# Windowed attention feeding a dense layer: attention in groups of 128 queries with four-tile scores, instead of tiles of 64

## The chip, the cores and the metric

The kernel runs on one core of one Trainium2 chip. The metric is the device time of one execution in microseconds. Before the change three runs gave 781.32, 781.82 and 783.75 us, with a median of 781.82.

The core has a matrix engine (TensorE, PE; its weight loads are counted apart as PEld), a vector engine (VectorE, DVE), an activation engine (ScalarE, ACT), GpSimd (POOL) and SyncE (SP), which here issues all DMAs of data.

## The reference

There are 4 batches, 8 heads, 768 tokens and a head size of 64. Each query sees the keys less than 16 tokens away, and one summary per block of 32 tokens: the maximum of the keys and the mean of the values. The attention's result, 3072 x 512, goes through a gated layer of width 1536:

```
k_sum = k.reshape(B, H, 24, 32, D).max(axis=3)
v_sum = v.reshape(B, H, 24, 32, D).mean(axis=3)
scores_l = where(abs(i - j) < 16, scale * q @ k.T, -1e9)
scores_s = scale * q @ k_sum.T + log(32)
a = softmax(concat(scores_l, scores_s))
x = (a @ concat(v, v_sum)).transpose(0, 2, 1, 3).reshape(3072, 512)
out = ((x @ w_a) * (x @ w_b)) @ w_out
```

q, k and v are fp32. The weights come as 64-bit floats and are converted on the chip.

## The kernel before, in words

**The dense layer.** The 3072 tokens are 12 units u of 256 rows, three to a batch. The hidden width is 12 blocks f of 128. A pair (u, f) is an item; there are 144. `hidden` multiplies the unit's x by a block of w_a and of w_b (`up`, 12 matmuls of 128x256 each, L487; three products per 128 rows, since x and the weights are split into a high and a low part). ACT copies the first product to SBUF (L521), DVE multiplies the second into it (L522, the tensor g), ACT rounds g to its high part gh (L525), POOL makes the low part gl (L526). `down` then adds g @ w_out to the unit's two PSUM banks po with 6 matmuls of 128x512 (L504). It runs one item late: the program issues the up matmuls of item i, then the down matmuls of item i - 1. The PSUM tile h of an item has two buffers, so the up matmuls of an item wait for the g of two items before.

**Order of the items.** Units 0 and 1 are interleaved (five items of unit 0, then one of unit 1 and one of unit 0 in turn), because each item there also needs its weights converted: 36 conversions of 128x512 (L168 to L192) on ACT, DVE and POOL, each using two tiles of the pool `stage`, 7 buffers, and the PSUM tile psc. Units 2 to 11 follow one after the other.

**Attention.** `attention(u)` is a generator; the main loop takes its steps between the matmuls of the items of unit u - 1, spread evenly by `a_steps` (14 steps, or 20 for the first unit of a batch). All of unit 0's attention stands at the start. On every engine a scheduler then sets the final order.

A unit's 256 queries are 4 tiles of 64 (QT). Of a tile:
- `prep_q` turns q so that the head dimension lies on partitions and writes it to a block-diagonal tile qbd (two heads of 64 rows, zeros elsewhere); by DVE block transposes from a load in 32x32 blocks (L369), or, for units 0 to 2 (u < FILL), by TensorE and ACT copies (L367).
- `scores` multiplies it with 120 keys, 96 of the window and 24 summaries that lie between the window's two halves in the key tile kT: 4 matmuls of 128x120 on the full array (L385). DVE scales and masks (L391) and takes the maximum (L397), ACT does 4 exps (L399), DVE the reciprocal of the sums (L403, L404), POOL the division (L409).
- `transp` turns the weights of attention with 16 DVE transposes of 32x128 (L426), or for u < FILL on TensorE (L419), and the value sums are loaded into the value tile vw by a DMA.
- `av` multiplies with vw: 8 matmuls of 120x64, each in one half of the array's columns (L434). ACT and DVE write the high and low part of x (L439, L440).

`load_v` loads the window's values with two DMAs into vw (L375), which has two buffers. `prep_k` runs at the start of a batch: it loads keys in 32x32 blocks (L295), transposes them into kT (L327), takes block maxima (L328) and has POOL write the summaries between the windows (L332). `sum_v` (L229 to L237) makes the value means. All DMAs of the blocks of k and q wait for the last weight conversion.

Of the kernel before, what the change touches and what calls it, by code (L numbers as in the profile page):

```python
# [21 lines left out]
def attention_moe(  # L22
# [21 lines left out]
    KEYS = NS + WIN  # L44
    CH = 256
    NR = S // CH
    G = CH // QT
# [3 lines left out]
    stage = ctx.enter_context(tc.tile_pool(name="stage", bufs=7))  # L51
# [16 lines left out]
    PAIR = 2 * QT + NS  # L68

    def window(t):  # L70

        if t == 0:
            return 0, QT
        if t == S // QT - 1:
            return S - WIN, WIN - QT
        return QT * t - 16, 16 if t % 2 else WIN - 16

    def column(token):
        return PAIR * (token // (2 * QT)) + (QT + NS) * (token // QT % 2) + token % QT

    kinds = {0: 0, S // QT - 1: 3}
    mask = const.tile([P, 4, KEYS], F32, name="mask")
    nc.gpsimd.memset(mask, 0.0)
    for i, t in enumerate((0, 1, 2, S // QT - 1)):
        start, na = window(t)
        off = QT * t - start
        for h in range(2):
            hs = slice(h * QT, (h + 1) * QT)  # L90
            for c0, n, key in ((0, na, 0), (na + NS, WIN - na, na)):
                sl = mask[hs, i, c0 : c0 + n]

                for sign, base in ((1, 15 - off + key), (-1, 15 + off - key)):
                    nc.gpsimd.affine_select(
                        out=sl,
                        in_=sl,
                        compare_op=ALU.is_ge,
                        fill=NEG,
                        base=base,  # L100
                        pattern=[[sign, n]],
                        channel_multiplier=-sign,
                    )
        nc.gpsimd.memset(mask[:, i, na : na + NS], LOG32)


    qbds = []
    for i in range(2):
        t = const.tile([P, NP, P], F32, name=f"qbd{i}")
        nc.vector.memset(t, 0.0)  # L110
        qbds.append(t)
# [5 lines left out]

    sbufs = []
    for i in range(2):
        t = const.tile([P, NP, P], F32, name=f"s{i}")  # L120
        nc.gpsimd.memset(t[:, :, KEYS:], 0.0)
        sbufs.append(t)

# [72 lines left out]
    kTs, vsums = {}, {}  # L196
# [57 lines left out]
    def load_first():  # L254
# [14 lines left out]
        first["v"].append(att.tile([P, S], F32, tag="kin", name="v_in2", bufs=1)[:, :512])  # L269
        first["v"].append(stage.tile([P, 512], F32, tag="t2k", name="v_in3"))  # L270
        first["v"] += [att.tile([P, 512], F32, tag="pt", name=f"v_in{4 + i}") for i in range(2)]
# [14 lines left out]
    def blocks(dst, x, b, c, row):  # L286

        for h in range(2):
            for e in range(D // 32):
                src = x[b, 2 * c + h, row:, e * 32 :]
                r0 = 32 * (2 * h + e)
                load = nc.sync.dma_start(  # L295
                    out=dst[r0 : r0 + 32].rearrange("p (n d) -> p n d", d=32),
                    in_=bass.AP(
                        tensor=src.tensor,
                        offset=src.offset,
                        ap=[[D, 32], [32 * D, dst.shape[1] // 32], [1, 32]],  # L300
                    ),
                )
                tc.add_manual_dep(load.ins, converted[-1].ins.name, after, reason="pace")

    def prep_k(b, early):
        kT = att.tile([P, NP, S // P, PAIR], F32, tag="kT", name=f"kT{b}", bufs=1)
        ks = att.tile([P, NP, NS], F32, tag="ksum", name=f"ks{b}", bufs=1)
        n = P // BLK
        if early:
            for i in range(S // P):  # L310
                tr = turned(first["k"][i], f"k{i}", 0)
                nc.scalar.copy(out=kT[:, :, i, :QT], in_=tr[:, :, :QT])
                nc.scalar.copy(out=kT[:, :, i, QT + NS :], in_=tr[:, :, QT:])
# [6 lines left out]
        for c in range(NP):  # L320
            if not early:
                xin = att.tile([P, S], F32, tag="kin", name=f"kin{b}_{c}", bufs=1)
                blocks(xin, k, b, c, 0)
                xin = xin.rearrange("p (i e x) -> p e i x", e=2, x=QT)
                kv = ks[:, c, :].rearrange("p (i e n) -> p e i n", e=2, n=QT // BLK)
                for e, half in enumerate((kT[:, c, :, :QT], kT[:, c, :, QT + NS :])):
                    nc.vector.transpose(out=half, in_=xin[:, e])  # L327
                    nc.vector.tensor_reduce(  # L328
                        out=kv[:, e], in_=half.rearrange("p i (n x) -> p i n x", x=BLK),
                        axis=AX.X, op=ALU.max,  # L330
                    )
            nc.gpsimd.tensor_copy(  # L332
                out=kT[:, c, :, QT : QT + NS],
# [4 lines left out]
        kTs[b] = kT.rearrange("p c n x -> p c (n x)")  # L338
# [17 lines left out]
    def prep_q(u, i, qin):  # L356
        if u < FILL:
            x = turned(qin[:, i, :], f"q{u}_{i}", u)
        else:
            x = qin[:, :, i * P : i * P + P]  # L360
        for j in range(2):
            for h in range(2):
                hs = slice(h * D, (h + 1) * D)
                dst = qbds[j][hs, :, h * QT : (h + 1) * QT]
                src = x[hs, :, j * QT : (j + 1) * QT]
                if u < FILL:
# [46 lines left out]
    def transp(b, t, u):  # L413
# [10 lines left out]
        for qs in blk:  # L424
            for ks in blk:
                nc.vector.transpose(out=ptv[ks, :, qs], in_=s[qs, :, ks])  # L426
# [187 lines left out]
```

## Time and profile before

| what | value |
|---|---|
| median of three runs | 781.82 us (781.32 to 783.75) |
| the profiled execution | 783.04 us, span 781.2 us |
| mean granted TensorE clock | 0.984 |
| PE busy | 726.3 us, 93% of the span |
| DVE busy | 505.7 us, 65% |
| ACT busy | 278.1 us, 36% |
| POOL busy | 250.6 us, 32% |
| first item's matmuls start | 48.7 us |
| first items of units 2, 3 and 11 | 189.8, 256.7 and 728.2 us |

The starts of units are those of the first w_a or w_b run of their item 0 in the trace. The time of an execution is 1.8 us longer than its span. Busy PE time contains some overlap and some modelled ends, so times of matmuls are better read from the start of one run to the start of the next in the timeline. A group of instructions is printed as line, engine, operation, output<-inputs, sizes and count, then its total busy time and the mean ns of one, then the idle time just before and what ended it. A wait is printed as engine and tile, what it waited for, and total us, times, longest.

### The profile page before, as it was taken

The numbers are of one execution on the slowest core, as the hardware profiler recorded it, in microseconds if no ns is written. First come the engines' busy times: TensorE is split into PE (matmuls) and PEld (weight loads), VectorE is DVE, ScalarE is ACT, GpSimd is POOL, SyncE is SP. The second block draws the span as 40 slices with busy tenths as digits, with TensorE's granted clock in tenths as the row PEclk, the third lists the DMA queues.
The fourth block names the chain that finished last, engine by engine and source line by source line (L and its number), as shares of the span: only waits on it lengthen the run. The fifth ranks groups of instructions, "written<-read, shape, count | busy, mean of one in ns | idle before, by whom it ended". The sixth has DMA issues, their size and how long they took to land.

```text
span 781.2 us, 14975 instructions
## 1 busy us (share of the span) xinstructions
PE 726.3 (93%) x5580; PEld 655.4 (84%) x5580; DVE 505.7 (65%) x1262; ACT 278.1 (36%) x898; POOL 250.6 (32%) x328
## 2 busy tenths in 40 slices
PE   6668998999789999999999999999989999999997
PEld 4367888888678989988888989988988989989996
DVE  4779999834884664767867665667876656556100
ACT  4758965423222322322222422322223332322212
POOL 5567789921222212212222221222122221121111
PEclk9869999999999999999999999999999999999999
DMA  9965645246411211204521111114421111100000
GB/s 217 219 191 164 172 136 176 85 86 137 91 30 31 55 21 39 50 18 86 138 36 39 50 31 27 49 32 75 126 37 27 55 35 29 43 13 14 28 1 28
DMA packets 157129, 56.97 MB, mean 73 GB/s; under 512 B 136704, under 2 KB 148992, under 8 KB 157056
## 3 DMA queue, kind: packets, MB, share of 16 engines
q1 hardware_dynamic: 157056, 56.01, 29.8%
q8 instruction: 44, 0.72, 0.4%
q14 instruction: 29, 0.24, 0.1%
HBM read 47.19 MB, written 6.29 MB: 68 GB/s over the span
## 4 chain that ended last, share of the span: by engine, by line
PE 40%; DVE 33%; ACT 7%; POOL 5%; SPq 5%; DMA 4%; issue 4%; ACTq 0%; DVEq 0%; POOLq 0%
PE h L487 23%; DVE ptsb L426 15%; PE po L504 13%; ACT s L399 5%; POOL s L409 3%; DVE vp L230 3%; SPq L295 2%; DVE s L391 2%; DVE nml L397 2%; PE av L434 2%; DVE qbd L369 2%; PE s L385 2%; DMA kin<-in_k_dram 2%; DVE g L522 2%; DVE kT L327 1%
## 5 line engine op out<-in xcount | busy, mean ns | idle before, releaser
L487 PE MATMUL h<-x,w_a 128*128 128x256 f32 x1728 | 247.3, 284 | 15.4 <-DVE g L522 14.4
L487 PEld LDWEIGHTS h<-x,w_a 128*128 128x128 f32 x1728 | 231.3, 190 | 33.6 <-DVE g L522 17.9
L487 PE MATMUL h<-x,w_b 128*128 128x256 f32 x1728 | 225.4, 278 | 0.0
L487 PEld LDWEIGHTS h<-x,w_b 128*128 128x128 f32 x1728 | 211.7, 189 | 1.8 <-POOL w_b L192 0.2
L526 POOL TENSOR_TENSOR gl<-g,gh 128x256 fp32r<-128x256 f32 x144 | 106.0, 738 | 324.1 <-ACT gh L525 316.4
L426 DVE STREAM_TRANSPOSE ptsb<-s 32x128 f32<-32x128 f32 x576 | 174.3, 303 | 32.2 <-POOL s L409 23.3
L504 PE MATMUL po<-w_o,gh 128*128 128x512 f32 x576 | 171.6, 404 | 6.2 <-ACT gh L525 5.6
L522 DVE TENSOR_TENSOR g<-h,g 128x256 f32<-128x256 f32 x144 | 59.8, 419 | 116.1 <-ACT g L521 114.6
L525 ACT CAST gh<-g 128x256 fp32r<-128x256 f32 x144 | 58.2, 407 | 182.5 <-DVE g L522 182.4
L504 PEld LDWEIGHTS po<-w_o,gh 128*128 128x128 f32 x576 | 97.7, 188 | 24.5 <-ACT gh L525 10.3
L521 ACT COPY g<-h 128x256 f32<-128x256 f32 x144 | 52.4, 369 | 171.0 <-PE h L487 169.2
L399 ACT ACTIVATE s<-s,nml 128x120 f32<-128x120 f32 x192 | 73.5, 384 | 91.5 <-DVE nml L397 91.4
L504 PE MATMUL po<-w_o,gl 128*128 128x512 f32 x288 | 100.1, 398 | 0.7 <-POOL gl L526 0.2
L409 POOL TENSOR_TENSOR s<-s,nml 128x480 f32<-128x480 f32 x40 | 39.5, 988 | 106.6 <-DVE nml L404 67.8
L385 PE MATMUL s<-kT,qbd 128*128 128x120 f32 x384 | 53.8, 283 | 8.6 <-DVE s L391 3.4
L385 PEld LDWEIGHTS s<-kT,qbd 128*128 128x128 f32 x384 | 50.1, 197 | 12.0 <-DVE s L391 3.8
L504 PEld LDWEIGHTS po<-w_o,gl 128*128 128x128 f32 x288 | 49.1, 188 | 9.3 <-POOL gl L526 2.9
L403 DVE TENSOR_SCALAR nml<-nml 128x4 f32<-128x4 f32 x48 | 12.2, 254 | 52.7 <-ACT s L399 52.7
L391 DVE SCALAR_TENSOR_TENSOR s<-s,mask 128x480 f32<-128x480 f32 x48 | 31.2, 653 | 20.4 <-PE s L385 20.0
L434 PEld LDWEIGHTS av<-ptsb,vw 120*64 120x64 f32 x768 | 28.4, 144 | 17.6 <-issue 7.5
L434 PE MATMUL av<-ptsb,vw 120*64 120x64 f32 x768 | 35.6, 236 | 7.7 <-DMA vw<-in_v_dram 4.2
L399 ACT ACTIVATION_READ_ACCUMULATOR s<-s,nml 128x1 f32 x192 | 35.9, 187 | 0.0
(67 smaller groups left out, 507.1 us busy)
## 6 DMA issues: line engine op xcount, KB each, us to landing
vw<-in_v_dram SPq DMA_DIRECT2D x40, 160.0 KB
raw_a<-in_moe_w_a_dram SPq DMA_DIRECT2D x12, 512.0 KB
raw_b<-in_moe_w_b_dram SPq DMA_DIRECT2D x12, 512.0 KB
raw_o<-in_moe_w_out_dram SPq DMA_DIRECT2D x12, 512.0 KB
out_dram<-ob SPq DMA_DIRECT2D x24, 256.0 KB
kin<-in_k_dram SPq DMA_DIRECT2D x48, 96.0 KB
qin<-in_q_dram SPq DMA_DIRECT2D x144, 32.0 KB
vb<-in_v_dram SPq DMA_DIRECT2D x24, 192.0 KB
```

Source lines behind the costliest of these rows:

```text
L385: nc.tensor.matmul(ps[:, c, :], qbds[t % 2][:, c, :], kTs[b][:, c, c0 : c0 + KEYS], start=True, stop=True,)
L391: nc.vector.scalar_tensor_tensor(out=s, in0=ps, scalar=0.125, in1=mask[:, kind, None, :].broadcast_to([P, NP, KEYS]), op0=ALU.mult, op1=AL ...
L399: nc.scalar.activation(s[:, c, :], s[:, c, :], AF.Exp, bias=nm[:, c : c + 1], scale=1.0, accum_out=l[:, c : c + 1],)
L409: nc.gpsimd.tensor_tensor(out=s, in0=s, in1=l[:, :, None].broadcast_to([P, NP, KEYS]), op=ALU.mult)
L426: nc.vector.transpose(out=ptv[ks, :, qs], in_=s[qs, :, ks])
L434: nc.tensor.matmul(ps[h * D : (h + 1) * D, c, :], vw[:KEYS, 2 * c + h, :], pt[:KEYS, q0 : q0 + QT], start=True, stop=True, tile_position=( ...
L487: nc.tensor.matmul(ps, wts[nm, f][:, c, part, :], x[xpart][:, c, :], start=(i == 0), stop=(i == n - 1))
L504: nc.tensor.matmul(po[j], g[:, js], w[:, 0, part, :], start=(f == 0 and i == 0), stop=(f == NF - 1 and i == 2),)
L521: nc.scalar.copy(out=g, in_=pa)
L522: nc.vector.tensor_tensor(out=g, in0=pb, in1=g, op=ALU.mult)
L525: nc.scalar.copy(out=gh, in_=g)
L526: nc.gpsimd.tensor_tensor(out=gl, in0=g, in1=gh.bitcast(F32), op=ALU.subtract)
```

## The change

The unit's 256 queries become 2 groups of 128 (G = CH // P). The pieces:
- The score matmuls use 64x64 tiles of the array. The row half is the head of a pair (h), the column half is the half of the queries (e). A group needs 16 matmuls 64x128 (L423) instead of 2 x 4 of 128x120, into two PSUM banks, one for each h. qbd is gone; q is turned by one transpose (L376) or one copy (L374) a group.
- Keys lie in kT with a period of 160 for 128 tokens: a window of 96 keys, a block of 32 with the 24 summaries, and again 32 keys, so that the summaries and the parts of the windows are aligned to 32. A query half e reads 128 columns: of these, one block of 32 is never needed by a given block of 32 queries.
- The softmax of a group is over two banks: 2 masks (L430), 2 maxima (L436), 8 exps (L441), 2 reciprocals (L446, L447), 2 products on POOL (L452).
- `transp` has 12 transposes of 32x256 (L472) a group instead of 2 x 16 of 32x128.
- `av` has 16 matmuls (L480) a group, the same columns as before, with a value tile for each e (vw0, vw1).
- Fixed single buffers s, pt, vw0, vw1 and kin replace pool tiles; unit 0 uses stage tiles for its second group's scores and values. The pool `stage` has 6 buffers instead of 7. The value tile is loaded by 3 DMAs a group (L395); the value sums are loaded twice a batch (L402).
- `prep_k` has three transposes a chunk (L325 to L327), three maxima over half blocks of 16 (L332, L336) and two joins (L340, L344).
- A unit has 8 steps of attention (14 for the first of a batch) instead of 14 (20), in the order scores, transposes of the group before, scores of the next, av.

```diff
-    stage = ctx.enter_context(tc.tile_pool(name="stage", bufs=7))
+    stage = ctx.enter_context(tc.tile_pool(name="stage", bufs=6))
...
+    sbuf = const.tile([P, 2, NP, P], F32, name="s")
+    pbuf = const.tile([P, 2, NP, P], F32, name="pt")
+    vbuf = [const.tile([P, H, D], F32, name=f"vw{e}") for e in range(2)]
...
+        qT = att.tile([P, NP, P], F32, tag="qT", name=f"qT{u}_{i}")
         if u < FILL:
-            x = turned(qin[:, i, :], f"q{u}_{i}", u)
+            nc.scalar.copy(out=qT, in_=turned(qin[:, i, :], f"q{u}_{i}", u))
         else:
-            x = qin[:, :, i * P : i * P + P]
...
+            nc.vector.transpose(out=qT, in_=qin[:, :, i * P : (i + 1) * P])
...
-            nc.tensor.matmul(
-                ps[:, c, :], qbds[t % 2][:, c, :], kTs[b][:, c, c0 : c0 + KEYS],
-                start=True, stop=True,
-            )
...
+        order = [(c, h) for c in range(NP) for h in range(2)]
+        if u == 2:
+            order.sort(key=lambda x: x[1])
+        for c, h in order:
...
+            for e in range(2):
+                es = slice(e * QT, (e + 1) * QT)
+                c0 = PER * t + QT * e
+                nc.tensor.matmul(
+                    banks[h][es, c, :], qT[hs, c, es], kT[hs, c, c0 : c0 + P],
+                    start=True, stop=True, tile_position=(h * D, e * QT),
+                )
...
-        blk = [slice(i * 32, (i + 1) * 32) for i in range(P // 32)]
-        ptv = pt.rearrange("p (c x) -> p c x", x=P)
-        for qs in blk:
-            for ks in blk:
-                nc.vector.transpose(out=ptv[ks, :, qs], in_=s[qs, :, ks])
...
+        for i, ks in enumerate(((0, 1, 3), (1, 2, 3), (0, 1, 2), (1, 2, 3))):
+            qs = slice(32 * i, 32 * (i + 1))
+            for j in ks:
+                js = slice(32 * j, 32 * (j + 1))
+                nc.vector.transpose(out=pv[js, :, qs], in_=sv[qs, :, js])
...
+            for e in range(2):
+                es = slice(e * QT, (e + 1) * QT)
+                for h in range(2):
+                    nc.tensor.matmul(
+                        ps[h * D : (h + 1) * D, c, es], vw[e][:, 2 * c + h, :], pbuf[:, h, c, es],
+                        start=True, stop=True, tile_position=(0, h * D),
+                    )
...
+        vw = load_v(b, t0)
+        qT = prep_q(u, 0, qin)
+        yield
+        scores(u, t0, qT, s)
+        yield
+        qT = prep_q(u, 1, qin)
+        yield
...
+        transp(u, t0, s)
+        yield
+        if u:
+            scores(u, t1, qT, s1)
+            yield
+        av(u, t0, vw, xs[u])
+        yield
+        if u:
+            vw1 = load_v(b, t1)
+        transp(u, t1, s1)
+        yield
+        av(u, t1, vw1, xs[u])
+        yield
```

How the order moves, at three places. In the names of before, s2_4 is batch 2, tile 4; in those of after, s7_2_0 is unit 7, group 2 of its batch, head half 0; po5, g6 and h6 carry the unit, and gh5_10 the unit and block. The first place is VectorE at the start, where unit 0's softmax meets the first weight conversions. Before:

```order
L170 TENSOR_SCALAR s_a0_465<-p_a0_464 128x512
L173 SCALAR_TENSOR_TENSOR f_a0_463<-p_a0_464,s_a0_465 128x512
L179 TENSOR_SCALAR s_a0_465<-f_a0_463 128x512
L182 SCALAR_TENSOR_TENSOR p_a0_464<-raw_a0_219,s_a0_465 128x512
L391 SCALAR_TENSOR_TENSOR s0_199<-s0_0_298,mask_87 128x4x120
L391 SCALAR_TENSOR_TENSOR s1_201<-s0_1_316,mask_87 128x4x120
L170 TENSOR_SCALAR s_b0_479<-p_b0_478 128x512
```

And after:

```order
L430 SCALAR_TENSOR_TENSOR s_171<-s0_0_0_275,mask_94 128x512
L430 SCALAR_TENSOR_TENSOR s_171<-s0_0_1_278,mask_94 128x512
L436 TENSOR_REDUCE nml0_0_293<-s_171 128x4 x2
L446 TENSOR_SCALAR nml0_0_293<-nml0_0_293 128x4
L447 RECIPROCAL nml0_0_293<-nml0_0_293 128x4
L446 TENSOR_SCALAR nml0_0_293<-nml0_0_293 128x4
L447 RECIPROCAL nml0_0_293<-nml0_0_293 128x4
L430 SCALAR_TENSOR_TENSOR s1_0_263<-s0_1_0_319,mask_94 128x512
L430 SCALAR_TENSOR_TENSOR s1_1_264<-s0_1_1_322,mask_94 128x512
L436 TENSOR_REDUCE nml0_1_337<-s1_0_263 128x4
L161 TENSOR_SCALAR s_a0_442<-p_a0_441 128x512
```

Before, the first conversion (L170 to L182) stands ahead of unit 0's first masks; after, it stands behind the first group's whole softmax and the masks of the second.

The second place is TensorE late in unit 5's items, where attention of the next units goes between the down matmuls. Before:

```order
L434 MATMUL av2_3_5104<-ptsb2_3_5037,vw2_3_4914 64x64 x8
L504 MATMUL po5_0_4469<-w_o10_1442,gh5_10_5033 128x512 x2
L504 MATMUL po5_0_4469<-w_o10_1442,gl5_10_5034 128x512
L504 MATMUL po5_1_4470<-w_o10_1442,gh5_10_5033 128x512 x2
L504 MATMUL po5_1_4470<-w_o10_1442,gl5_10_5034 128x512
L385 MATMUL s2_4_5191<-kT2_4393,qbd0_189 128x120 x4
L487 MATMUL h6_0_5121<-x6_0_4536,w_a0_471 128x256
```

And after:

```order
L480 MATMUL av6_1_4887<-pt_172,vw0_173 64x64 x2
L423 MATMUL s7_2_0_5012<-kT_87,qT7_0_4966 64x128
L480 MATMUL av6_1_4887<-pt_172,vw1_174 64x64 x2
L480 MATMUL av6_1_4887<-pt_172,vw0_173 64x64 x2
...
L569 MATMUL po5_0_4304<-w_o10_1409,gh5_10_4830 128x512 x2
L569 MATMUL po5_0_4304<-w_o10_1409,gl5_10_4831 128x512
L569 MATMUL po5_1_4305<-w_o10_1409,gh5_10_4830 128x512 x2
L569 MATMUL po5_1_4305<-w_o10_1409,gl5_10_4831 128x512
L423 MATMUL s7_2_0_5012<-kT_87,qT7_0_4966 64x128 x7
L569 MATMUL po5_0_4304<-w_o11_1485,gh5_11_4883 128x512 x2
```

Before, av and scores of a tile each stand in one run. After, a score matmul of the next group stands between av's matmuls, and the seven others of that head half come later, on their own; the eight of the other half come later still.

The third place is VectorE in the steady stretch. Before:

```order
L403 TENSOR_SCALAR nml2_4_5197<-nml2_4_5197 128x4
L404 RECIPROCAL nml2_4_5197<-nml2_4_5197 128x4
L522 TENSOR_TENSOR g6_0_5146<-h6_0_5121,g6_0_5146 128x256
L426 STREAM_TRANSPOSE ptsb2_4_5296<-s0_199 32x4x32 x16
L522 TENSOR_TENSOR g6_1_5231<-h6_1_5206,g6_1_5231 128x256
```

And after:

```order
L446 TENSOR_SCALAR nml7_2_5030<-nml7_2_5030 128x4
L447 RECIPROCAL nml7_2_5030<-nml7_2_5030 128x4
L587 TENSOR_TENSOR g6_2_5082<-h6_2_5057,g6_2_5082 128x256
L472 STREAM_TRANSPOSE pt_172<-s_171 32x8x32 x12
L587 TENSOR_TENSOR g6_3_5120<-h6_3_5095,g6_3_5120 128x256
```

The run of transposes between two products g is 12 wide ones instead of 16, and it comes once for 128 queries instead of once for 64.

More of the change, by code (lines that the diff above doesn't have):

```diff
@@ L107, in attention_moe @@
[L107 to L111, printed above, removed]
+    PER = 160
+    KC = (S // P) * PER + 32
+    kT = const.tile([P, NP, KC], F32, name="kT")
+    nc.gpsimd.memset(kT[:, :, :16], 0.0)
+    nc.gpsimd.memset(kT[:, :, KC - 16 :], 0.0)
+    kper = kT[:, :, : KC - 32].rearrange("p c (i x) -> p c i x", x=PER)
+    for c in range(NP):
+        nc.gpsimd.memset(kper[:, c, :, WIN + NS : WIN + 32], 0.0)
@@ L193, in convert_weights @@
             yield f, nm
-    kTs, vsums = {}, {}
+    vsums = {}
     psum_pools = {
@@ L268, in load_first @@
         first["v"] = [t[:, i, :] for i in range(2)]
-        first["v"].append(att.tile([P, S], F32, tag="kin", name="v_in2", bufs=1)[:, :512])
+        first["v"].append(kin[:, :512])
         first["v"].append(stage.tile([P, 512], F32, tag="t2k", name="v_in3"))
-        first["v"] += [att.tile([P, 512], F32, tag="pt", name=f"v_in{4 + i}") for i in range(2)]
+        first["v"] += [pbuf[:, i].rearrange("p c x -> p (c x)") for i in range(2)]
         for nm, i in (
@@ L371, in load_v @@
-    def load_v(b, t):
-        vw = att.tile([P, H, D], F32, tag="vw", name=f"vw{b}_{t}")
-        start, na = window(t)
-        for r0, key, rows in ((0, 0, na), (na + NS, na, WIN - na)):
+            nc.vector.transpose(out=qT, in_=qin[:, :, i * P : (i + 1) * P])
+        return qT
+    def load_v(b, t, spare=False):
+        if spare:
+            vw = [stage.tile([P, H, D], F32, tag="t2k", name=f"vw{b}_{t}_{e}") for e in range(2)]
+            nc.gpsimd.memset(vw[0][WIN:], 0.0)
+            nc.gpsimd.memset(vw[1][32:64], 0.0)
+        else:
+            vw = vbuf
+        row = t * P
+        skip = 16 if t == 0 else 0
+        end = min(row + P + 16, S)
+        for e, r0, lo, hi in (
+            (0, skip, row - 16 + skip, row + 80),
+            (1, 0, row + 48, row + 80),
+            (1, 64, row + 80, end),
+        ):
@@ L413, in transp @@
-    def transp(b, t, u):
-        s = sbufs[t % 2]
-        pt = att.tile([P, NP * P], F32, tag="pt", name=f"ptsb{b}_{t}")
-        if u < FILL:
-            ps = psum(f"pt{b}_{t}", u)
-            for c in range(NP):
-                nc.tensor.transpose(ps[:KEYS, c * P : (c + 1) * P], s[:, c, :KEYS], ident)
-            nc.scalar.copy(out=pt[:KEYS], in_=ps[:KEYS])
-            return pt
-        blk = [slice(i * 32, (i + 1) * 32) for i in range(P // 32)]
-        ptv = pt.rearrange("p (c x) -> p c x", x=P)
-        for qs in blk:
-            for ks in blk:
-                nc.vector.transpose(out=ptv[ks, :, qs], in_=s[qs, :, ks])
-        return pt
@@ L429, in av @@
[L429 to L438 removed]
+                out=vw[e][r0 : r0 + hi - lo], in_=v[b, :, lo:hi, :].rearrange("h p d -> p h d")
+            )
```

268 lines of the change are left out of this document (141 added, 127 removed).

## The prediction

> **What bounds the kernel now.** I read the busy totals first, then the stretches between the units' starts, then TensorE's timeline with and without attention, its waits, and the groups of VectorE.
>
> ```profile
> span 781.2 us, 14975 instructions
> PE 726.3 (93%) x5580; PEld 655.4 (84%) x5580; DVE 505.7 (65%) x1262; ACT 278.1 (36%) x898; POOL 250.6 (32%) x328
> 189.80:256.70 66.90, 58.88 (x458) 53.32 (x458) 47.81 (x122) 16.22 (x61) 13.66 (x19) 1.00 0.29 62
> 256.70:728.20 471.50, 459.99 (x3641) 420.87 (x3641) 310.96 (x876) 138.33 (x496) 105.00 (x140) 1.00 0.21 46
> 728.20:781.20 53.00, 48.91 (x351) 45.17 (x350) 5.09 (x12) 11.30 (x28) 8.83 (x12) 1.00 0.06 21
> ```
>
> The columns behind the bounds of a stretch are its length and the busy time of PE, PEld, DVE, ACT and POOL. The second stretch is units 3 to 10, 96 items with the attention of units 4 to 11 in them: TensorE is busy for 460.0 of 471.5 us at full clock. So only less TensorE work, or fewer of its waits, can move the end there. The last stretch is unit 11 without attention, and shows what a bare item costs:
>
> ```profile
> 742.34 1.55 PE L487 MATMUL h<-x,w_a 128*128 128x256 f32 x12
> 743.72 1.52 PE L487 MATMUL h<-x,w_b 128*128 128x256 f32 x12
> 745.08 1.08 PE L504 MATMUL po<-w_o,gh 128*128 128x512 f32 x4
> 746.00 0.62 PE L504 MATMUL po<-w_o,gl 128*128 128x512 f32 x2
> 746.46 0.98 PE L487 MATMUL h<-x,w_a 128*128 128x256 f32 x7
> ```
>
> From start to start an item takes 746.46 - 742.34 = 4.12 us: 1.38 for w_a, 1.36 for w_b, 0.23 for each of six down matmuls. The same stretch of code with attention in it:
>
> ```profile
> 462.38 1.52 PE L487 MATMUL h<-x,w_b 128*128 128x256 f32 x12
> 463.83 0.69 PE L434 MATMUL av<-ptsb,vw 120*64 120x64 f32 x16
> 464.45 0.74 PE L504 MATMUL po<-w_o,gh 128*128 128x512 f32 x2
> 465.03 0.40 PE L504 MATMUL po<-w_o,gl 128*128 128x512 f32 x1
> 465.96 1.05 PE L385 MATMUL s<-kT,qbd 128*128 128x120 f32 x8
> 466.77 1.62 PE L487 MATMUL h<-x,w_a 128*128 128x256 f32 x12
> 468.22 1.52 PE L487 MATMUL h<-x,w_b 128*128 128x256 f32 x12
> ```
>
> An av tile takes 0.62 us to the next start; the w_b run ahead of it is 0.09 longer than bare (463.83 - 462.38 - 1.36) and the two down matmuls behind it 0.12 (465.03 - 464.45 - 0.46): 0.83. A score tile takes 0.81, and the w_a behind it is 0.07 longer: 0.88. Together 1.71 us for 64 queries, 54.7 for the 32 tiles of units 4 to 11. Items make 96 x 4.12 = 395.5. Of the 471.5 us there remain 21.3, of which the waits name about half:
>
> ```profile
> PEld po L504 <- ACT gh L525: 9.6, 19, 1.3
> PEld h L487 <- DVE g L522: 6.3, 8, 0.9
> PE po L504 <- ACT gh L525: 5.6, 7, 1.1
> PE h L487 <- DVE g L522: 4.8, 8, 0.7
> ```
>
> All are waits for an item's g, 10.4 us by the matmuls and 15.9 by their weight loads (one wait can show in both). g goes from ACT (L521) through DVE (L522) to ACT (L525), and what DVE has queued ahead of it is mostly the attention's transposes:
>
> ```profile
> L426 DVE STREAM_TRANSPOSE ptsb<-s 32x128 f32<-32x128 f32 x576 | 174.3, 303 | 32.2 <-POOL s L409 23.3 <-PE av L434 1.2
> L391 DVE SCALAR_TENSOR_TENSOR s<-s,mask 128x480 f32<-128x480 f32 x48 | 31.2, 653 | 20.4 <-PE s L385 20.0
> L369 DVE STREAM_TRANSPOSE qbd<-qin 64x256 f32<-64x256 f32 x72 | 31.2, 434 | 3.3 <-DMA qin<-in_q_dram 2.6
> L397 DVE TENSOR_REDUCE nml<-s 128x4 f32<-128x480 f32 x48 | 31.1, 649 | 1.1
> L399 ACT ACTIVATE s<-s,nml 128x120 f32<-128x120 f32 x192 | 73.5, 384 | 91.5 <-DVE nml L397 91.4
> L409 POOL TENSOR_TENSOR s<-s,nml 128x480 f32<-128x480 f32 x40 | 39.5, 988 | 106.6 <-DVE nml L404 67.8 <-ACT g L521 35.3 <-ACT gh L525 1.8
> ```
>
> **The change, TensorE.** The price of a small fp32 matmul can be read where two passes of 512 columns follow each other at the start:
>
> ```profile
> 21.29 0.10 PEld L212 LDWEIGHTS vs<-v_in,mean 128*24 128x24 f32 x1 [0.33 <-issue]
> 21.72 0.10 PEld L212 LDWEIGHTS vs<-v_in,mean 128*24 128x24 f32 x1 [0.33 <-issue]
> ```
>
> 0.43 us for 512 columns is 0.84 ns a column, and each fp32 matmul is two passes (16 rows for 8 matmuls of av). The score tile agrees: 8 x 120 x 0.84 ns = 0.81. The 16 av passes of 64 columns would take 0.86 one after the other, yet took 0.62; so the two column tiles overlap. If wholly, they need 0.43, and 0.83 - 0.43 = 0.40 us is what a run of tiled matmuls costs for going in and out. "TensorE: Matmul & The Clock Gate" (the Trainium skill, section The mechanism) says that a weight load overlaps running matmuls only where its rows of the array are others. Av's column tiles share all rows, so by that rule its 0.62 could not lie under 0.86; here the trace differs.
>
> After, a group of 128 queries issues 32 score passes of 128 columns (0.107 us each) in four tiles, and 32 av passes of 64 columns in two. With all four tiles at work the scores take 8 x 0.107 + 0.40 = 1.26; av takes 16 x 0.054 + 0.40 = 1.26. That is 2.52 against 2 x 1.71 = 3.42: 0.90 less a group, 14.4 over the 16 groups of units 4 to 11. The scheduler's order takes most of it back. It breaks score and av groups into pieces between the down matmuls, some ten more than whole groups would give per batch of 6 groups, each going in and out of tiles again (10 x 0.40 = 4.0), and issues one or two groups with all of one half's heads ahead of the other's, where only pairs can overlap (about 1.1). 5.1 x 16/6 = 13.6. **Term: -1 us.** Bounds: -14 if going in and out is free of cost between pieces; +11 if only pairs ever overlap (below).
>
> **VectorE.** Per unit, 64 block transposes at 0.303 (19.4 us) become 24 of twice the width; nearest row 0.434 (64x256): 10.4. Eight qbd transposes at 0.434 (3.5) become 2 of 128x512; between 0.434 and the 0.69 of a 128x512 operation (L182, below), I take 0.69: 1.4. Mask and maximum grow from 480 to 512 columns, +0.4. Sum -10.7 of about 36 us of attention work per unit. A run of transposes is 16 x 0.303 = 4.85 before and 12 x 0.434 = 5.2 after, but there are 2 per unit instead of 4, so g is caught behind one half as often. I take half of the 15.9 us of waits: **-8 us**. Bounds: 0, if each of the fewer runs catches g for twice as long, and -21, if all that is left of the stretch was due to it. Unit 2's own attention work, in the 66.9 us stretch: an eighth, **-1**.
>
> **ACT and POOL.** The eight exps of a group stand in one row, 8 x 0.384 = 3.07 us, ahead of a copy of g. From the end of w_b to the down matmul that needs its gh lie 4.1 us (the next item), and the chain of g takes some 1.2, so 2.9 are free: at worst 0.2 per group shows, under 4 in all. The two POOL products (2 x 0.99) are covered likewise. Costed at nothing.
>
> **Loads.** v takes 3 DMAs a group instead of 4, and the block sums go in twice a batch instead of 12 times.
>
> ```profile
> SPq L375 <- PE av L434: 221.6, 39, 25.5
> 42.06 4.94 DMA vw<-vs
> 174.55 2.75 DMA kin<-in_k_dram
> 186.52 4.18 DMA kin<-in_k_dram
> ```
>
> The first row says that SP waited already for av to free its buffer, 221.6 us of it, with the later q and k blocks queued behind and TensorE unharmed. Single buffers make that wait longer: the next group's v is issued only behind av of the one before, and lands 2.75 to 4.94 us later. The order puts two items, 8.2 us, between two av. Covered; with the cover gone, some 3 us per group.
>
> k takes one more pass per chunk on DVE:
>
> ```profile
> L327 DVE STREAM_TRANSPOSE kT<-kin 128x384 f32<-128x384 f32 x24 | 12.4, 555 | 15.0 <-DMA kin<-in_k_dram 15.0
> L328 DVE TENSOR_REDUCE ks<-kT 128x12 f32<-128x384 f32 x24 | 11.9, 531 | 0.0
> ```
>
> Before 2 x (0.555 + 0.531) = 2.17 us; after, the same 768 columns in pieces of 576, 192 and 32 and two small maxima, an estimate of 2.7 from these rows. +2 a batch on DVE, hidden.
>
> **Start.** These rows are the 2nd, 6th and last weight conversion on DVE, and TensorE's first item:
>
> ```profile
> 22.21 0.69 DVE L182 SCALAR_TENSOR_TENSOR p_b<-raw_b,s_b 128x512 f32<-128x512 uint32 x1
> 42.88 0.69 DVE L182 SCALAR_TENSOR_TENSOR p_o<-raw_o,s_o 128x512 f32<-128x512 uint32 x1
> 154.09 0.69 DVE L182 SCALAR_TENSOR_TENSOR p_o<-raw_o,s_o 128x512 f32<-128x512 uint32 x1
> 48.72 3.17 PE L487 MATMUL h<-x,w_a 128*128 128x256 f32 x13 [0.46 <-ACT x L439]
> ```
>
> Before, av of unit 0 waits for the sums' DMA (42.06 + 4.94 = 47.0), and the first item starts at 48.7. After, unit 0 has its own buffers for both groups, so one landing serves both: the first item some 7 us earlier. But five of the six stage buffers (before: one of seven) are taken by unit 0, and each conversion needs two. The second must then wait until the first group's softmax frees some, about 39 instead of 22.9 us, and the sixth some 10 later than 43.6. From there conversions run at their own pace, so the last ends about 162, not 154.8, which delays batch 1's k blocks behind it, and unit 2 with them, by some 2; its lighter DVE work gives as much back. **Term 0**, bounds -8 (first item early, conversions catch up) and +16 (39 - 22.9, none regained).
>
> **Sum.** -1 - 8 - 1 + 0 = -10 on the profiled 783.04 us (span 781.2 and 1.8 around it): 773.0. The median of the runs, 781.82, lies 1.2 lower; on its scale 772.
>
> **The rivals**, on the median's scale.
> - *Only pairs overlap* (0.15). Av's 0.62 us proves two tiles, nothing shows four. Scores then cost 16 x 0.107 + 0.40 = 2.12, +0.86 for each of 16 groups less the 2.9 already counted: +11, so 782, no change. The rule of the Trainium skill that is named above would give the same: the two query tiles of one head share their rows.
> - *Going in and out of four tiles costs more than of two* (0.10), slower. Some 11 score pieces a batch make 29 here; at 1.2 us each instead of 0.40 that is +23: 795. It decides from 0.40 + 10/29 = 0.75 us a piece. For it: rows and columns are both split now; against: av's switch is cheap. "TensorEngine Tiling (Array Packing)" (the Trainium skill, section Key Properties) says that changing the tiling mode drains TensorE; av's 0.40 is what one such change shows here, and no run shows one with four tiles.
> - *The start pays and never regains* (0.17): the 15 us of late conversions stay, since items of units 0 and 1 need new weights each: 772 + 15 = 787. For it: 36 conversions follow one another with little idle time up to 154.8. Against: the window to 256.7 has TensorE idle for 8 of 66.9 us.
> - *DVE was behind all that is left of the stretch* (0.13): -21 in place of -8, 759.
>
> **How the numbers follow.** 772 has 0.45. The range runs from 757, just beyond the last rival, to 788, just beyond the start's; it leaves out the dearer tiles and parts of the tails. About 0.3% (2.35 us) is what a measurement of this kernel can tell from none. Faster by more: 0.45 + 0.13, and 0.07 from the kind ends of pairs and start, 0.65. Same: most of the pairs' 0.15, 0.12. Slower: 0.10 from tiles, 0.12 from the start, 0.01 from pairs, 0.23.
>
> **What would show it.** Right: the scores of a whole group take about 0.9 us to the next start, av about 1.0, DVE's attention work falls by about 10 us a unit, waits for g halve, and units 3 to 10 take some 462 us instead of 471.5. Wrong: 1.7 us for whole scores; score pieces of over 0.75 us for a few matmuls; unit 2's first item well after 195 us; TensorE waiting for v's DMA; or waits for g as long as before with half as many runs of transposes.

## The result, and the profile after

The changed kernel takes 756.92 us (median of 4 runs, 756.20 to 759.98), beside 782.66 for the kernel before (its three runs given above and a fourth): the ratio is 0.9679, with a 95% interval from 0.9647 to 0.9712. The prediction said 772, between 757 and 788. The sign is right; the gain is more than twice the forecast, 25.7 us instead of 10, and the time lies just under the range. One of the four runs of a_spare, below, took 3910.47 us for a reason that no trace shows; its ratio leaves that run out.

The profiled execution took 756.2 us, with a span of 754.3 against 781.2. The top of its page:

```profile
span 754.3 us, 15201 instructions
PE 718.0 (95%) x5964; PEld 644.0 (85%) x5964; DVE 410.6 (54%) x870; ACT 275.9 (37%) x856; POOL 254.2 (34%) x333
```

Its stretches at the same places as before (unit 2, units 3 to 10, unit 11):

```profile
191.70:250.90 59.20, 57.46 (x474) 51.89 (x473) 33.04 (x64) 16.30 (x54) 12.63 (x17) 1.00 0.27 66
250.90:700.40 449.50, 448.02 (x3884) 409.68 (x3884) 227.84 (x528) 138.02 (x478) 107.15 (x140) 1.00 0.20 44
700.40:754.30 53.90, 49.85 (x356) 45.95 (x354) 5.09 (x12) 11.40 (x28) 8.84 (x12) 1.00 0.06 21
```

Unit 2 begins 1.9 us later than before (191.7 against 189.8), takes 7.7 us less (59.2 against 66.9), units 3 to 10 take 22.0 less (449.5 against 471.5), unit 11 takes 0.9 more: together -26.9, the difference of the spans. In units 3 to 10 TensorE is idle for 1.5 us where it was idle for 11.5, and busy for 448.0 instead of 460.0. VectorE has 83.1 us less to do there, 10.4 a unit.

TensorE's timeline in the middle of that stretch, with a group's scores and a group's av in one run each:

```profile
447.02 1.10 PE L423 MATMUL s<-kT,qT 64*64 64x128 f32 x32
448.06 0.73 PE L569 MATMUL po<-w_o,gh 128*128 128x512 f32 x2
...
452.38 1.15 PE L480 MATMUL av<-pt,vw 128*64 128x64 f32 x32
453.46 0.74 PE L569 MATMUL po<-w_o,gh 128*128 128x512 f32 x2
```

The 32 score passes take 1.04 us to the next start, the 32 av passes 1.08. Of TensorE's waits in that stretch, these are the longest that are left:

```profile
PEld po L569 <- issue: 2.9, 17, 0.2
PEld av L480 <- DVE pt L472: 1.8, 2, 1.0
PEld h L552 <- issue: 1.5, 9, 0.2
PE av L480 <- DVE pt L472: 1.3, 2, 0.8
```

No wait of a matmul for g is left, where before 10.4 us stood under these names. The groups of VectorE that the prediction had priced from other shapes:

```profile
L472 DVE STREAM_TRANSPOSE pt<-s 32x256 f32<-32x256 f32 x216 | 94.3, 436 | 11.4 <-POOL s L452 8.4 <-PE av L480 0.2
L376 DVE STREAM_TRANSPOSE qT<-qin 128x512 f32<-128x512 f32 x18 | 12.5, 700 | 0.7 <-DMA qin<-in_q_dram 0.7
```

What changed can be seen at one place of each kernel. Before, on VectorE, ScalarE and TensorE (rows between them left out):

```profile
449.44 0.37 ACT L521 COPY g<-h 128x256 f32<-128x256 f32 x1 [0.35 <-PE h L487]
449.51 5.04 DVE L426 STREAM_TRANSPOSE ptsb<-s 32x128 f32<-32x128 f32 x16 [0.85 <-POOL s L409]
...
454.58 0.42 DVE L522 TENSOR_TENSOR g<-h,g 128x256 f32<-128x256 f32 x1
...
455.06 0.38 PE L487 MATMUL h<-x,w_a 128*128 128x256 f32 x1 [0.68 <-DVE g L522]
```

A run of 16 transposes starts just as the copy for g does, and g, which stands behind the run in VectorE's order, starts at 454.58, 4.77 us after the copy's end. TensorE runs out of work. After:

```profile
455.50 5.40 DVE L472 STREAM_TRANSPOSE pt<-s 32x256 f32<-32x256 f32 x12 [0.18 <-POOL s L452]
...
457.97 0.37 ACT L586 COPY g<-h 128x256 f32<-128x256 f32 x1 [2.94 <-PE h L552]
...
460.93 0.42 DVE L587 TENSOR_TENSOR g<-h,g 128x256 f32<-128x256 f32 x1
```

The run is a little longer, but it began 2.5 us ahead of the copy, and g is 2.6 us late, without a wait of TensorE behind it. Why the scheduler's order puts the run there was not tested. Counted over the trace (start of an item's product on VectorE less the end of its copy on ScalarE), of the 96 items in units 3 to 10 g starts over 4 us late 17 times before and 2 times after, over 3 us late 28 and 8 times.

### The profile page after: what moved, and what is told of

It is laid out like the page before. It is cut to its first block, busy times and chain, and to the rows that moved or that the text cites. A ratio compares the mean times of both kernels' runs of the same rounds, so it can differ in the third digit from the quotient of the medians.

```text
span 754.3 us, 15201 instructions
## 1 busy us (share of the span) xinstructions
PE 718.0 (95%) x5964; PEld 644.0 (85%) x5964; DVE 410.6 (54%) x870; ACT 275.9 (37%) x856; POOL 254.2 (34%) x333
## 4 chain that ended last, share of the span: by engine, by line
PE 70%; DVE 14%; POOL 5%; DMA 5%; issue 2%; SPq 2%; ACT 1%; ACTq 0%; DVEq 0%; POOLq 0%
PE h L552 40%; PE po L569 22%; PE s L423 4%; PE av L480 2%; DMA kin<-in_k_dram 2%; SPq L293 1%; DVE pt L472 1%; PE vs L203 1%; DVE s_b L161 1%; POOL f_b L182 1%; POOL w_b L183 1%; DVE kT L325 1%; DVE f_a L164 1%; DVE vp L221 1%; DVE p_a L173 1%
## 5 line engine op out<-in xcount | busy, mean ns | idle before, releaser
L552 PE MATMUL h<-x,w_a 128*128 128x256 f32 x1728 | 242.1, 283 | 6.8 <-DVE g L587 6.7
L472 DVE STREAM_TRANSPOSE pt<-s 32x256 f32<-32x256 f32 x216 | 94.3, 436 | 11.4 <-POOL s L452 8.4
L441 ACT ACTIVATE s<-s,nml 128x128 f32<-128x128 f32 x192 | 74.6, 390 | 40.4 <-DVE nml L436 40.4
L452 POOL TENSOR_TENSOR s<-s,nml 128x512 f32<-128x512 f32 x40 | 41.6, 1041 | 98.7 <-DVE nml L447 93.5
L569 PEld LDWEIGHTS po<-w_o,gl 128*128 128x128 f32 x288 | 51.1, 190 | 9.2 <-POOL gl L591 1.0
L430 DVE SCALAR_TENSOR_TENSOR s<-s,mask 128x512 f32<-128x512 f32 x48 | 31.8, 683 | 25.2 <-PE s L423 23.2
L423 PE MATMUL s<-kT,qT 64*64 64x128 f32 x768 | 43.2, 286 | 1.0 <-POOL kT L348 0.8
L423 PEld LDWEIGHTS s<-kT,qT 64*64 64x64 f32 x768 | 31.0, 137 | 9.0 <-issue 1.4
L480 PE MATMUL av<-pt,vw 128*64 128x64 f32 x768 | 31.5, 231 | 5.2 <-DMA vw<-vs 3.8
L446 DVE TENSOR_SCALAR nml<-nml 128x4 f32<-128x4 f32 x48 | 10.7, 223 | 46.9 <-ACT s L441 46.9
L441 ACT ACTIVATION_READ_ACCUMULATOR s<-s,nml 128x1 f32 x192 | 36.0, 187 | 0.0
L480 PEld LDWEIGHTS av<-pt,vw 128*64 128x64 f32 x768 | 26.8, 142 | 10.4 <-ACT s L441 4.0
```

Of the source, the lines that this page charges most:

```text
L423: nc.tensor.matmul(banks[h][es, c, :], qT[hs, c, es], kT[hs, c, c0 : c0 + P], start=True, stop=True, tile_position=(h * D, e * QT),)
L430: nc.vector.scalar_tensor_tensor(out=s[h], in0=banks[h], scalar=0.125, in1=mask[:, kind, None, :].broadcast_to([P, NP, P]), op0=ALU.mult, ...
L441: nc.scalar.activation(s[h][:, c, :], s[h][:, c, :], AF.Exp, bias=nml[:, 0, h, c : c + 1], scale=1.0, accum_out=nml[:, 1, h, c : c + 1],)
L452: nc.gpsimd.tensor_tensor(out=s[h], in0=s[h], in1=l[:, :, None].broadcast_to([P, NP, P]), op=ALU.mult)
L472: nc.vector.transpose(out=pv[js, :, qs], in_=sv[qs, :, js])
L480: nc.tensor.matmul(ps[h * D : (h + 1) * D, c, es], vw[e][:, 2 * c + h, :], pbuf[:, h, c, es], start=True, stop=True, tile_position=(0, h * D),
```

## The experiments

Two theories. **V**: TensorE was waiting because g stood behind transposes on VectorE; the change shortened VectorE's work. **P**: the gain is TensorE's own work, cheaper scores and fewer runs of small matmuls. V later split in two: **L**, a long run ahead of a g decides, and **S**, VectorE's load as a sum decides. A run of score or av matmuls, on TensorE, is a stretch of one of the two kinds without other matmuls between; where such runs are counted against 63 the attention of units 3 to 11 is meant, and in units 3 to 10 alone the trace has 54 of them in the changed kernel and 67 in the one before. Of each kernel the row of units 3 to 10 (its own starts of units 3 and 11) is shown where the verdict rests on it.

**VectorE's transposes of before in the changed kernel** (a_tr32).

```diff
-        for i, ks in enumerate(((0, 1, 3), (1, 2, 3), (0, 1, 2), (1, 2, 3))):
-            qs = slice(32 * i, 32 * (i + 1))
-            for j in ks:
-                js = slice(32 * j, 32 * (j + 1))
-                nc.vector.transpose(out=pv[js, :, qs], in_=sv[qs, :, js])
+        for h in range(2):
+            for i in range(4):
+                qs = slice(32 * i, 32 * (i + 1))
+                for j in range(4):
+                    js = slice(32 * j, 32 * (j + 1))
+                    nc.vector.transpose(
+                        out=pv[js, h * NP : (h + 1) * NP, qs], in_=sv[qs, h * NP : (h + 1) * NP, js]
+                    )
```

> The changed kernel, with each group's transposes cut as before the change: 32 of 32x128 (9.7 us by the row of before, 0.303 each) in place of 12 of 32x256 (5.2). VectorE's attention work is then as long per unit as before the change, while TensorE's work stays that of the changed kernel. Theory V (TensorE waited for g because VectorE was busy with transposes; their shortening took away the 10.0 us of TensorE idle time in units 3 to 10 and 6.3 in unit 2): most of it comes back, +8 to +16 us on 756.9, 765 to 773. Theory P (what was gained is TensorE's own work, cheaper scores and fewer runs of small matmuls): at most +3, 757 to 760.

Measured: 799.03 us, ratio to before 1.0203 (1.0179 to 1.0227), 42 us over the changed kernel and some 2% slower than the kernel before.

```profile
255.30:741.60 486.30, 467.94 (x3883) 422.79 (x3882) 298.96 (x848) 136.38 (x476) 107.65 (x140) 0.98 0.18 41
```

And two of TensorE's waits in it:

```profile
PE h L555 <- DVE g L590: 10.7, 10, 2.5
PE av L483 <- DVE pt L473: 3.9, 7, 1.2
```

V holds, P doesn't, and V was itself too low: VectorE's load is below that of before (299.0 against 311.0), but TensorE is idle for 18.4 us, more than before. A group's transposes take 9.7 us instead of 5.2, in pieces of at most 7.3 us with other VectorE work between them. What VectorE does from one g to the next is over 7 us ten times, up to 10.4, where in the changed kernel it is at most 5.9; g is over 5 us late in 13 of 96 items, which before it was in none. So the 36.8 us that this stretch is longer than in the changed kernel are not all waits: 16.9 are idle time, some 10 are the granted clock of 0.98 (486.3 x 0.02; see the last section), and TensorE's order has 70 runs of small matmuls instead of 54, some 6 us by the 0.4 us a run that is worked out under a_tr6.

**The kernel before with half of its transposes** (b_tr8). The same with one in four (b_tr4) has `blk[:1]`. Both take fixed buffers for the result.

```diff
         for qs in blk:
-            for ks in blk:
+            for ks in blk[:2]:
                 nc.vector.transpose(out=ptv[ks, :, qs], in_=s[qs, :, ks])
```

> The kernel before the change, which leaves out 8 of the 16 block transposes of each tile from unit 3 on (fixed buffers for their results, so that nothing else has to fill them): VectorE has 9.7 us less per unit, as by the change, and TensorE has the same work as before. Theory V: the waits for g mostly go, -10 to -16 us on 782.7: 767 to 773. Theory P: -3 to 0, 780 to 783.

Measured: 762.07 us, ratio 0.9729 (0.9707 to 0.9751), a larger gain than V's range had.

> The kernel before the change, which leaves out 12 of the 16 block transposes of each tile from unit 3 on, where the run with 8 left out gave 762.1. If that run had reached the floor that TensorE's work of before sets (1.7 us idle in 455.8): 759 to 762, and the difference from the changed kernel's floor is what TensorE's own work gained, 4 to 7 us. If VectorE's load still counted there: 750 to 757, and TensorE's own gain is nearly nothing.

Measured: 757.66, ratio 0.9686 (0.9666 to 0.9707), between the two ranges. The first row is that of b_tr8:

```profile
252.20:708.00 455.80, 454.13 (x3643) 420.02 (x3643) 234.30 (x620) 141.62 (x496) 105.66 (x140) 1.00 0.21 48
```

```profile
250.10:703.40 453.30, 453.05 (x3643) 419.96 (x3642) 196.86 (x492) 142.23 (x496) 105.65 (x140) 1.00 0.21 48
```

With VectorE's load near that of the changed kernel (234.3 against 227.8) and TensorE's work as before, units 3 to 10 take 455.8 instead of 471.5. So VectorE's part of the 22.0 us is 15.7, or 18.2 where all of its waits go (453.3). TensorE's own part is what remains, 6.3 or 3.8. (b_tr8 has the load of the changed kernel, but in twice as many runs of half the length.)

**The changed kernel with half of its twelve transposes** (a_tr6), to find its floor.

```diff
-        for i, ks in enumerate(((0, 1, 3), (1, 2, 3), (0, 1, 2), (1, 2, 3))):
+        for i, ks in enumerate(((0,), (1, 2), (0, 1), (3,))):
```

> The changed kernel, which leaves out six of the twelve block transposes of each group from unit 3 on; TensorE's work stays the same. If VectorE no longer decides in the changed kernel (1.5 us of idle TensorE in the 449.5 us of units 3 to 10, 1.7 in unit 2): 754 to 757, and this is the floor that TensorE's own work sets. If VectorE still delays TensorE in ways that the waits don't show: under 751.

Measured: 749.17 us, ratio 0.9584 (0.9559 to 0.9608), under the first range: VectorE still cost time in the changed kernel that its waits don't show.

```profile
250.50:692.50 442.00, 442.00 (x3884) 406.75 (x3883) 186.52 (x432) 138.78 (x477) 107.29 (x140) 1.00 0.20 45
```

The stretch is 7.5 us shorter, though only 1.5 us of idle time were there to remove. The scheduler's order explains most of the rest: it has 50 runs of score and av matmuls instead of 63 (42 instead of 54 in the stretch). Summed from the trace (from start to start, idle time left out, and with what the matmuls next to them take longer), the small matmuls take 46.6 us of that stretch instead of 51.6 for the same work. That is about 0.4 us for each run saved, the price that the prediction took. VectorE's load thus acts through the order too, and the split above depends on what is taken off first: with each kernel at its lightest VectorE load, TensorE's part would be 11.3 us (453.3 in b_tr4 against 442.0).

**Two tiles instead of four** (a_pairs).

```diff
-        if u == 2:
-            order.sort(key=lambda x: x[1])
+        order.sort(key=lambda x: x[1])
```

> The changed kernel, with the score matmuls of a group in another order in all units: all eight of the first head half, then all eight of the second. Two tiles of the same rows can then overlap, but not four. If four tiles do overlap in the changed kernel (its whole groups take 1.04 us to the next start), a whole group's scores take 16 x 0.107 + 0.2 = 1.9 us: +0.86 for each of the some ten to sixteen groups of units 4 to 11 that are not in halves already, 766 to 771. If only pairs ever overlap, nothing changes: 756 to 759.

Measured: 757.5 us, ratio 0.9673 (0.9651 to 0.9695): no change in the whole, as if only pairs ever overlapped. But the rows say otherwise:

```profile
253.50:700.60 447.10, 447.10 (x3884) 412.03 (x3883) 229.46 (x528) 141.14 (x477) 107.26 (x140) 1.00 0.20 45
448.14 1.59 PE L422 MATMUL s<-kT,qT 64*64 64x128 f32 x32
449.66 0.73 PE L568 MATMUL po<-w_o,gh 128*128 128x512 f32 x2
```

The same 32 passes take 1.52 us instead of 1.04: four tiles do overlap in the changed kernel. Even here it is not pairs alone, which would need 16 x 0.107 = 1.71 us: in the trace two passes start every 0.11 us, but four between 448.64 and 448.96, where the halves meet. That is why less was lost than expected. What the groups lose is given back because this order has 50 runs instead of 63, every av group in one run, and no idle time (447.1 us for units 3 to 10). The time alone would have led to the wrong verdict.

**An order between the two** (a_mix): half of the rounds can use four tiles. In a_mix4 it holds from unit 4 on only.

```diff
         if u == 2:
             order.sort(key=lambda x: x[1])
+        else:
+            order = [(0, 0), (1, 0), (2, 0), (0, 1), (3, 0), (1, 1), (2, 1), (3, 1)]
```

> The changed kernel, with the score matmuls ordered so that the first head half starts three pairs of columns ahead of the second: half of the rounds can use four tiles, and the first bank is done early. The order has 48 runs of score and av matmuls from unit 3 on instead of 63 (50 where the halves are apart). If the number of runs costs what it did in the stretch (some 0.3 us each, 4 to 5 us) and the lost overlap some 0.2 us a group (3.5): 754 to 757. If the overlap alone counts: 758 to 761.

Measured: 756.05, ratio 0.9668 (0.9634 to 0.9701): the same as the changed kernel. Units 3 to 10 took 444.7 us, but unit 2 61.6.

> The changed kernel with the mixed order of score matmuls from unit 4 on only, unit 3 as in the changed kernel (with the mixed order unit 2, which holds unit 3's attention, took 61.6 us instead of 59.2, and units 3 to 10 444.7 instead of 449.5). If the two add up: 445 us and 59 us, 751 to 754, faster than the changed kernel by over 0.3%. If unit 2's difference is not the order's: 754 to 757.

Measured (with `elif u > 3`): 752.1 us, ratio to before 0.9608 (0.9584 to 0.9632), whose interval lies under that of the changed kernel.

```profile
251.40:695.60 444.20, 444.20 (x3884) 409.66 (x3884) 229.52 (x528) 140.03 (x478) 107.47 (x140) 1.00 0.20 45
```

TensorE is never idle there. Unit 2 took 61.8 us, not 59, but it began at 189.6; by the start of unit 3 the two parts did add up, 251.4 here, 250.9 in the changed kernel and 253.2 in a_mix. Of the kernels that do all of the work this is the fastest.

**VectorE's load, spread** (a_spread).

```diff
         nc.vector.tensor_tensor(out=g, in0=pb, in1=g, op=ALU.mult)
+        if 3 <= u < NU - 1:
+            load = moe.tile([P, 2], F32, tag="load", name=f"load{u}_{f}")
+            nc.vector.tensor_reduce(
+                out=load, in_=g[:, None, :].broadcast_to([P, 2, CH]), axis=AX.X, op=ALU.max
+            )
```

> The changed kernel with VectorE's load of before, but spread: behind each item's g of units 3 to 10 a maximum over it whose result is not used (512 columns, 0.67 us by the row of the group maxima; 96 x 0.67 = 64 us, where the narrow transposes added 71). If what makes TensorE wait is one long run of transposes that a g is queued behind (theory L, the run's length against the some 3 us that an item leaves), the time stays near 756.9; the order has 74 runs of score and av matmuls instead of 63, at 0.4 us each +4, so 757 to 763. If VectorE's load as a sum decides (theory S): 780 to 800, as with the narrow transposes (799).

Measured: 761.62 us, ratio 0.9736 (0.9715 to 0.9756).

```profile
251.20:704.20 453.00, 451.04 (x3883) 410.64 (x3882) 289.96 (x624) 137.61 (x477) 107.39 (x140) 1.00 0.20 44
```

VectorE is busy for 290.0 us, nearly as with the narrow transposes (299.0), yet TensorE is idle for 2.0 us and not 18.4. The 4.7 us over the changed kernel are about what the eleven runs more cost. S falls: VectorE's share of busy time alone doesn't decide. L is borne out as far as what VectorE does from one g to the next is at most 6.4 us here. The maxima do delay g, though: it is over 4 us late in 8 items, where in the changed kernel it was in 2.

**A run of 16 wide transposes** (a_tr16).

```diff
-        for i, ks in enumerate(((0, 1, 3), (1, 2, 3), (0, 1, 2), (1, 2, 3))):
+        for i, ks in enumerate(((0, 1, 2, 3),) * 4):
```

> The changed kernel with all 16 wide block transposes of a group instead of 12: a run of 16 x 0.436 = 7.0 us instead of 5.2, and +3.5 us a unit on VectorE (28 in units 3 to 10, less than half of what the spread maxima add). Theory L: runs pass what two items leave, waits for g come back, +5 to +12: 762 to 769. Theory S: by the share of the load, 28/71 of 42 us: +17, 774.

Measured: 761.97 us, ratio 0.9742 (0.9703 to 0.9780), at the lower edge of L's range.

```profile
251.30:704.70 453.40, 450.34 (x3883) 411.65 (x3883) 255.10 (x592) 137.82 (x478) 107.44 (x140) 1.00 0.20 44
```

Runs of 7.0 us bring 3.1 us of idle time, where 5.2 brought 1.5. Most of the rest is TensorE's order: the small matmuls, summed as under a_tr6, take 54.7 us instead of 51.6. Adding 27 us to VectorE in longer runs costs as much as adding 62 us in short pieces. The length of a run is not the whole rule: the longest piece of a_tr32, with 18.4 us idle, is 7.3 us against 7.2 here, but from one g to the next VectorE does up to 10.4 us of work there and up to 7.7 here. TensorE's idle time goes better with how often g is over 4 us late, which is 17 times in a_tr32 (18.4 us idle) and before (11.5), 8 in a_spread (2.0), 7 here (3.1) and 2 in the changed kernel (1.5); VectorE's load, in the same order 299, 311, 290, 255 and 228 us, goes with it less well.

**The runs of before cut in two** (b_cut): each tile's 16 transposes are given out in two steps, with four steps more per unit.

```diff
-                pts[t - 1] = transp(b, t - 1, u)
+                pts[t - 1], todo = transp(b, t - 1, u)
+                blocks_of(todo[:8])
+                if u >= FILL:
+                    yield
+                blocks_of(todo[8:])
```

> The kernel before the change, with each tile's 16 block transposes given out in two steps of the attention, eight and eight: VectorE and TensorE have all of their work, and the order puts some of the runs' rests behind the next g (where the kernel before has 16 in one run in front of it). Theory L: fewer items whose g starts over 4 us late (17 of 96 in units 3 to 10 before), and the time falls by something like that share of the 16 to 19 us: 770 to 778. Theory S: 781 to 784.

Measured: 789.87 us, ratio 1.0085 (1.0065 to 1.0105), outside both ranges. The edit didn't do what it was meant to: the scheduler put most of the halves side by side again. g is over 4 us late in 16 items instead of 17, and units 3 to 10 have 12.8 us of idle time instead of 11.5:

```profile
258.90:735.70 476.80, 464.00 (x3641) 421.74 (x3640) 311.47 (x877) 138.40 (x494) 104.83 (x140) 1.00 0.20 46
```

The order has 81 runs of small matmuls in that stretch instead of 67; summed as under a_tr6 they take 63.8 us instead of 60.8, 3.0 of the 5.3 us that the stretch is longer. This run does not tell L and S apart.

**The start** (a_spare): unit 0's second scores and values in buffers of late weights.

```diff
-            s1 = [
-                stage.tile([P, 512], F32, tag="t2k", name=f"s1_{h}").rearrange(
-                    "p (c x) -> p c x", x=P
-                )
-                for h in range(2)
-            ]
+            spare = wp.tile([P, 2, NP, P], F32, tag=f"wo{NF - 1}", name="s1")
+            s1 = [spare[:, h] for h in range(2)]
...
-            vw = [stage.tile([P, H, D], F32, tag="t2k", name=f"vw{b}_{t}_{e}") for e in range(2)]
+            spare = wp.tile([P, 2, H, D], F32, tag=f"wb{NF - 1}", name=f"vw{b}_{t}")
+            vw = [spare[:, e] for e in range(2)]
```

> The changed kernel, with unit 0's second scores and values in the buffers of the last weights (which are loaded some 100 us later) instead of four of the six stage buffers. If the stage buffers are what delays the conversions at the start (second one done at 37.9 us instead of 22.9, last one at 158.0 instead of 154.8), the second is done by 24 us again, the last by 150, unit 2 starts 4 to 8 us earlier than at 191.7, and the time is 749 to 753. If conversions or items at the start are bound by something else (weights' loads, VectorE): 755 to 758.

Measured: 756.35 us, ratio 0.9654 (0.9625 to 0.9683): no change. The second conversion is done at 22.1 us instead of 37.9, so the stage buffers did delay the first ones; but the last ends at 157.1 instead of 158.0, unit 2 begins at 189.0, 2.7 earlier, and unit 3 at 251.0, as in the changed kernel (250.9). The stage buffers were not what sets the end of the start. In a_vbq, a_mix4, a_spread, a_tr16 and a_tr6 too unit 3 begins between 250.5 and 251.7 us, wherever unit 2 began (189.6 to 194.1); what holds it there was not found.

**The loads for the block sums on another queue** (a_vbq).

```diff
-            nc.sync.dma_start(out=vb, in_=vv[:, i * T : (i + 1) * T, :])
+            nc.scalar.dma_start(out=vb, in_=vv[:, i * T : (i + 1) * T, :])
```

> The changed kernel, with the loads of v for the block sums issued on ScalarE's queue instead of SyncE's, where they stand behind 48 blocks of q and k. In unit 2 the sums on VectorE wait for them, and the items' g stand behind the sums (unit 2 takes 59.2 us against 53.7 of unit 3). If that queue is the cause: unit 2 shorter by 2 to 5 us and 752 to 755. If the loads wait for something else, or ScalarE loses as much by issuing them: 756 to 759.

Measured: 759.79 us, ratio 0.9713 (0.9680 to 0.9746), just above the second range and not clear of the changed kernel. Unit 2 took 57.6 us instead of 59.2 but began 2.4 later, at 194.1; ScalarE has the loads between its copies of g. Nothing is won.

## Why the prediction was wrong

**The step that failed** is VectorE's: "I take half of the 15.9 us of waits: -8 us", and with it unit 2's "an eighth, -1". In place of 8, VectorE's part of units 3 to 10 is 15.7 to 18.2 us (b_tr8, b_tr4). Two things were wrong in it. The half came from counting runs of transposes, 2 per unit instead of 4, while TensorE's waits went with how often a g is caught for long: over 4 us late 17 times in the stretch before, 2 times after, an eighth. (Before, the 16 transposes of a tile did not always stand in one run either: the 32 tiles of the stretch have 50 pieces.) And the waits that the view names, 10.4 or 15.9 us, were taken for all that VectorE cost, although 21.3 us of the stretch were left over. With the load gone, 3.1 of these remain (453.3 - 395.5 - 54.7). The remainder was the better measure, and its rival, "DVE was behind all that is left of the stretch", at 759 with a chance of 0.13, is nearly what happened to this term; that the total came near its time is in part chance, since TensorE and unit 2 gave the rest.

**TensorE's own work**: -1 was forecast, 4 to 6 us were gained by difference. A sum of the small matmuls, as under a_tr6, comes near the lower end: 54.7 us in b_tr4 and 51.6 in the changed kernel. Its parts held: whole groups take 1.04 and 1.08 us to the next start, and with the neighbours' delay 1.24 and 1.30 where 1.26 was worked out for each; a further run costs about 0.4 us, as taken. The order has some eight more runs per batch than whole groups (54 for 16 groups, so 22 x 6/16), not ten.

**Unit 2** gained 7.7 us instead of 1, or 3 with the 2 that the start's term had its lighter VectorE work give back. b_tr8 gains 3.3 there (63.6 us) by VectorE alone, although its clock stands at 0.50 for 3.4 us of it, which it does not in the other two; how the rest divides between VectorE, the order, the sums' loads and TensorE was not settled.

**The start** came as worked out: the second conversion is done at 37.9 us (39 was expected), the sixth at 55.0 (some 10 later than 43.6), the last at 158.0 (162), the first item starts at 39.9 instead of 48.7, and unit 2 1.9 us later (2). The rival that the start never regains its loss fell: 15.0 us at the second conversion had become 3.2 at the last.

**VectorE's terms** held: 10.4 us less per unit (10.7 was expected), 0.436 us for a wide transpose (0.434), 0.700 for q's (0.69).

**The rivals of TensorE** both fell. (The first one's 782 should read 783, 772 + 11; its verdict of no change stays.) Four tiles overlap (1.04 against 1.52 us), and a piece of scores costs about 0.4 us around it, not 0.75. The rule of the Trainium skill ("TensorE: Matmul & The Clock Gate", The mechanism), that a weight load overlaps running matmuls only where its rows differ, doesn't fit here either: even the order with the head halves apart takes 1.52 us for 32 x 0.107 = 3.4 us of passes, most of which follow one on the same rows.

**The single value buffers** cost TensorE no wait that shows: no wait of TensorE for v's DMA stands in the stretch.

## What to carry to other kernels

When one engine is busy for 98% of a stretch, as here, work out what the stretch would take without any waits, and treat the whole remainder as open to a change that lightens the engine it waits for; the named waits were its lower end. Where an engine serves a short chain among long runs, in an order that is set beforehand, what stands ahead of one link of the chain matters more than the engine's share of busy time: 62 us more in short pieces cost 4.7, 71 us more in narrow transposes ahead of g cost 42, of which some 10 are the clock and some 6 TensorE's order. And a variant whose time does not change may still have changed two things: read the rows before giving a verdict.

## What the runs showed of the hardware

The clock of TensorE halved once it had been idle in a long-run variant. In a_tr32, at one such place:

```profile
361.10 2.92 PE L555 MATMUL h<-x,w_a 128*128 128x256 f32 x12 [2.50 <-DVE g L590]
```

The stretches of 3 us from there on, with the granted clock as the third number from the end:

```profile
361.00:364.00 3.00, 2.90 (x13) 2.90 (x14) 2.87 (x12) 0.68 (x2) 0.73 (x1) 0.50 0.65 104
364.00:367.00 3.00, 3.00 (x12) 2.61 (x11) 2.82 (x11) 0.41 (x1) 0.00 (x0) 0.50 0.00 0
367.00:370.00 3.00, 3.00 (x35) 2.59 (x35) 0.53 (x3) 0.78 (x2) 1.30 (x3) 0.98 0.03 8
```

After 2.50 us without work the clock stands at 0.50 for some 6 us, and the 12 matmuls take 2.92 us where they take 1.55 at full clock. So a wait of 2.5 us cost some 5.5: itself, and half of the 6 us. In the kernel before, an idle time of 3.39 us in unit 2 (219.38 to 222.77) was followed by a full clock; in b_cut one of 3.45 us at nearly the same place was followed by 0.50 from 221.4 to 228.2. So the length alone doesn't decide.

Shorter spells of 3.4 us at 0.50 stand in unit 2 of a_spare, a_mix4, b_tr8 and b_tr4, and not in that of the kernel before, the changed kernel or a_mix. Each costs some 1.7 us (an estimate: half of 3.4 with TensorE busy), so lengths of unit 2 should not be compared more finely than that.
